# Attention and a two-layer product on one core: the second product's work listed one step further ahead

## The chip, the cores and the metric

The kernel runs on one core of one Trainium2 chip. The metric is the device time of one execution, in microseconds (us). The kernel before has a median of 1421.46 us in 3 runs (1420.41 to 1422.7).

## The reference

An attention with a threshold, then two matrix products with an activation between them. B = 8 batches, 8 heads, 576 positions, head size 64; the 8 heads side by side give x with 4608 tokens and 512 columns.

```python
scores = scale * np.matmul(q, k.transpose(0, 1, 3, 2))
thresh = np.max(scores, axis=-1, keepdims=True) - tau
scores = np.where(scores >= thresh, scores, -1000000000.0)
...
x = np.ascontiguousarray(attn_out.transpose(0, 2, 1, 3)).reshape(B * S, H * D)
h = x @ w_in                                   # 4608 x 512 by 512 x 2048
sp = np.where(h > 20.0, h, np.log1p(np.exp(np.minimum(h, 20.0))))
g = h * np.tanh(sp)
return (g @ w_out).astype(np.float32)          # 4608 x 2048 by 2048 x 512
```

w_in and w_out reach the chip as 64-bit words and are decoded to fp32 there.

## The kernel before

Each fp32 operand of a matrix product is split into a high part, a cast, and a low part, the rest, and three matmuls (high by high, high by low, low by high) stand for one. So every operand costs a cast on ACT (names that end in h) and a subtraction on DVE (names that end in l).

The program has two parts. In the first, up to about 970 us, attention runs tile by tile, and the first product h = x w_in (gemm1, L553) is woven into it, one batch behind. Its results go through PSUM and a staging tile hst (L582, four slices, two buffers in the pool xpool) to DRAM (hd). For the last batch gemm1 runs alone, as 32 units of 12 matmuls (L798 to L805). Into these units a table (steps, from L782) puts the decode of w_out in eight parts j: load_w, convert (ACT), compose (three DVE operations and one POOL addition, tiles s and a), upper_w (ACT, tile w2h), lower_w (DVE, tile w2l). It also puts there the first loads, activations and splits of the second part.

The second part is the loop at L849: 72 steps n, nine token groups c of 512 tokens by eight parts j of the inner dimension. Step n needs these pieces of work:

- load_z(n): two loads of 256 KB from hd into a tile z, on the queue of SP. Five buffers of z take turns (CYCLE).
- combine(n): the activation Mish of z on ACT (ACTIVATE z<-z 128x1024); from group 1 on also a DVE subtraction (z<-z 128x512) and two POOL subtractions (z<-z 128x256 each), which form combinations of the features.
- split_z(n): the cast gh on ACT and the rest gl on DVE, 128x1024 in group 0 and 128x1792 after it. Three buffers of gh and gl take turns by n % 3: one in the pool er, two in the pool wl, which is opened when gemm1 has ended.
- in group 0 only, sums_w(n) (four DVE operations 128x256, two shown as z<-s, one as z<-z,s and one as z<-s,z) and split_w(n) (sh on ACT, sl on DVE): combinations of the decoded weight, formed once and used by all later groups. They lie in the second half of the tile z of step n.
- the matmuls. Group 0 is a plain product, 24 matmuls 128x512 in a step. From group 1 on, seven products (PRODUCTS, L42) of combined weights and combined features stand for eight: 42 matmuls 128x256 in a step, those with sh and sl among them.

Outputs are collected in PSUM over the eight steps of a group, in eight banks that are taken in turn (bank, L773): four for group 0, seven for each later group. At a group's last step leave (L816) copies the first product's bank to a tile c on ACT, adds the others to it and to its like on DVE (c<-o,c) and stores four results on the queue of SP. Group 0 has two copies on ACT and two on DVE instead. The tiles c come from the pool wl, in six buffers (held, L811).

The class InOrder (L81) makes the order in which the program lists its instructions the order in which each engine runs them. So an instruction that waits holds back all that is listed after it for its engine. Since every operation of PE, DVE, ACT and POOL is recorded in its helper, the profile puts them all on one line, L91, and they are told apart by tile names and shapes. In the changed kernel the helper stands on L92.

In the loop, the order of listing for one step was this: for n < 8 sums_w(n), split_z(n+1), split_w(n), combine(n+2), load_z(n+3) and then the matmuls of step n; from n = 9 on split_z(n+2), combine(n+3), load_z(n+4), matmuls. At n = 8 the lead grows by one step.

Of the kernel before, what the change touches and what calls it, by code (L numbers as in the profile page):

```python
# [5 lines left out]
F32 = mybir.dt.float32  # L6
# [8 lines left out]
P = 128  # L15
# [20 lines left out]
HB = S // 2  # L36
# [2 lines left out]
QT = 256  # L39
NG = B * S // (2 * QT) * NJ  # L40
CYCLE = (3, 4, 2, 0, 1)
PRODUCTS = ((0, 1), (4, 5), (5, 3), (3, 4), (6, 0), (2, 6), (1, 2))  # L42
QCOL = {
    0: [(0, 0)],
# [70 lines left out]
class Decode:  # L115
# [31 lines left out]
    def add(self):  # L147
        self.nc.gpsimd.tensor_tensor(self.a, self.b, self.c, ALU.add)
# [8 lines left out]
def attention_moe(tc, q, k, v, tau, w_in, w_out, out):  # L157
# [3 lines left out]
    with ExitStack() as outer:  # L161
# [8 lines left out]
        back = cst.tile([P, 1], F32, name="back")  # L170

        homes = {"zp": zp}
        words = {}
        wa = {}
        ws = {}
# [90 lines left out]
        with ExitStack() as first:  # L266
# [6 lines left out]
            with ExitStack() as att:  # L273
# [279 lines left out]
                def gemm1(b, xs, bank=shared, first=1):  # L553

                    halves = (range(NF // 2), range(NF // 2, NF))
                    if b < B - 1:
                        order = [(c, f) for c in range(2) for fs in halves for f in fs]  # L560
                    else:
                        order = [(c, f) for fs in halves for c in range(2) for f in fs]
                    banks = {}
                    made = {}

                    def parts(c, f, ds):
                        if (c, f) not in banks:
                            banks[c, f] = bank("h")
                        h = banks[c, f]
                        half, at = divmod(f * P, DF // 2)  # L570
                        for d in ds:
                            xh, xl = xs[d][c]
                            wh, wl = (w[:, d, at:at + P] for w in w1[half])
                            for i, (a, m) in enumerate(((wh, xh), (wh, xl), (wl, xh))):
                                nc.tensor.matmul(
                                    h[:, :HB], a, m, start=d == 0 and i == 0, stop=d == ND - 1 and i == 2
                                )
                                yield

                    def leave(c, f):  # L580
                        if f % 4 == 0:
                            made["hst"] = xpool.tile([P, 4, HB], F32, name="hst", bufs=2)  # L582
                        hst, h = made["hst"], banks.pop((c, f))
                        if b < B - 1 or f % 2:
                            nc.scalar.copy(hst[:, f % 4], h[:, :HB])
                        else:
                            nc.vector.tensor_copy(hst[:, f % 4], h[:, :HB])
                        if f % 4 == 3:
                            store(nc.sync if b < B - 1 else nc.scalar, hst, (2 * b + c) * HB, f - 3)

                    for c, f in order[:first]:
                        yield from parts(c, f, range(ND - 1))
                    for n, (c, f) in enumerate(order):
                        steps = parts(c, f, range(ND - 1, ND) if n < first else range(ND))
                        for i in range(3 if n < first else 3 * ND):
                            next(steps)
                            if i == (2 if n < first else 3 * ND - 1):
                                leave(c, f)
                            yield
# [179 lines left out]

            homes["wr"] = wr  # L780
            steps = {}
            for j in range(NJ):  # L782
                u = 4 * j
                steps.setdefault(u, []).append((compose, j))
                steps.setdefault(u + 2, []).append((upper_w, j))
                steps.setdefault(u + 3, []).append((lower_w, j))
                if j >= 3:
                    steps.setdefault(u - 10, []).append((load_w, j))
                    steps.setdefault(u - 3, []).append((convert, j))
            for n, u in enumerate((19, 20, 24, 28, 31)):  # L790
                steps.setdefault(u, []).append((load_z, n))
            for n, u in enumerate((22, 26, 30)):
                steps.setdefault(u, []).append((combine, n))
            steps.setdefault(24, []).append((split_z, 0))
            for _ in stream:
                pass
            stream = gemm1(B - 1, batches[B - 1], bank, 4)
# [11 lines left out]
        places = out.rearrange("(n p) t -> p n t", p=P)  # L809

        def held():  # L811
            return wl.tile([P, 2, QT], F32, name="c", tag="c", bufs=6)

        sums = {}

        def leave(k, c, o):  # L816

            def put(value, n, half):
                at = (2 * c + half) * QT
                nc.sync.dma_start(places[:, 2 * n:2 * n + 2, at:at + QT], value)  # L820

            def add(to, a, b, op=ALU.add):
                nc.vector.tensor_tensor(to, a, b, op)

            if k == 0:
                sums["c"] = held()
                nc.scalar.copy(sums["c"], o)
            elif k == 1:
                sums["u"] = held()
                add(sums["u"], o, sums["c"])  # L830
            elif k == 2:
                sums["v"] = held()
                add(sums["v"], o, sums["u"])
            elif k == 3:
                value = held()
                add(value, o, sums["v"])
                put(value, 1, 1)
                add(sums["u"], o, sums["u"])
            elif k == 4:
                add(sums["u"], o, sums["u"])  # L840
                put(sums["u"], 0, 1)
            elif k == 5:
                add(sums["v"], sums["v"], o, ALU.subtract)
                put(sums["v"], 1, 0)
            else:
                add(sums["c"], o, sums["c"])
                put(sums["c"], 0, 0)

        for n in range(NG):  # L849
            c, j = divmod(n, NJ)  # L850
            if n < NJ:
                sums_w(n)
            for i in range(n + 1 + (n > NJ + 1), n + 2 + (n > NJ)):
                split_z(i)
            if n < NJ:
                split_w(n)
            for i in range(n + 2 + (n > NJ), n + 3 + (n >= NJ)):
                if i > 2:
                    combine(i)
            for i in range(n + 3 + (n >= NJ), n + 4 + (n >= NJ - 1)):  # L860
                if i > 4:
                    load_z(i)
            if j == 0:
                banks = [bank("o") for _ in range(4 if c == 0 else len(PRODUCTS))]
            if c == 0:
                gh, gl = (x.rearrange("p n t -> p (n t)") for x in gs.pop(n))
                wh, wlo = wa[j]
                order = [(e, d) for e in range(2) for d in range(ND)]
                if j == NJ - 1:
                    order.sort(key=lambda at: at[1])  # L870
                for e, d in order:
                    cols = slice(2 * e * QT + d * P, 2 * e * QT + (d + 1) * P)
                    toks = slice(2 * e * QT, 2 * (e + 1) * QT)
                    for i, (x, y) in enumerate(((wh, gh), (wh, gl), (wlo, gh))):
                        nc.tensor.matmul(
                            banks[d], x[:, cols], y[:, toks],
                            start=j == e == i == 0, stop=j == NJ - 1 and e == 1 and i == 2,
                        )
                    if j == NJ - 1 and e == 1:
                        value = held().rearrange("p n t -> p (n t)")  # L880
                        if d % 2:
                            nc.vector.tensor_copy(value, banks[d])
                        else:
                            nc.scalar.copy(value, banks[d])
                        nc.sync.dma_start(out[d * P:(d + 1) * P, :2 * QT], value)
                continue
            for k, (wi, gi) in enumerate(PRODUCTS):
                o = banks[k].rearrange("p (n t) -> p n t", t=QT)
                w, at = (wa[j], (0, 2, 3)[wi]) if wi < 3 else (ws[j], wi - 3)
                for b in range(2):  # L890
                    cols = slice(at * QT + b * P, at * QT + (b + 1) * P)
                    for i, (x, y) in enumerate(((0, 0), (0, 1), (1, 0))):
                        nc.tensor.matmul(
                            o[:, b], w[x][:, cols], gs[n][y][:, gi],
                            start=j == b == i == 0, stop=j == NJ - 1 and b == 1 and i == 2,
                        )
                if j == NJ - 1:
                    leave(k, c, o)
            gs.pop(n)
# [46 lines left out]
```

## Time and profile before

| | before |
|---|---|
| median of 3 runs | 1421.46 us |
| profiled execution | 1421.81 us |
| its span | 1420.0 us |
| mean granted TensorE clock | 0.976 |
| PE busy | 1345.4 us, 95% |
| DVE busy | 1102.4 us, 78% |
| ACT busy | 990.0 us, 70% |
| POOL busy | 837.0 us, 59% |

PE is TensorE, DVE VectorE, ACT ScalarE, POOL GpSimd; SP issues DMAs. A row of the timeline has the start, the duration in us, engine, line, operation, the tile written and the tiles read, shapes, a count, and in brackets how long the engine was idle before it and what ended that. A row of the list of waits has engine, tile and line, what released it, the total in us, the number of waits and the longest. A row of the groups of instructions has the count after the x, then busy us and mean ns, then idle us and its releasers. Successive operations of an engine overlap a little in the records, so that the distance between starts is what a chain of them takes.

In forty equal slices of the span, PE's busy share and the granted clock stand like this:

```profile
PE   9998899999999999999999999997998889889888
PEclk9999999999999999999999999998999999999999
```

### The profile page before, as it was taken

The numbers are of one execution on the slowest core, as the hardware profiler recorded it, in microseconds if no ns is written. First come the engines' busy times: TensorE is split into PE (matmuls) and PEld (weight loads), VectorE is DVE, ScalarE is ACT, GpSimd is POOL, SyncE is SP. The second block draws the span as 40 slices with busy tenths as digits, with TensorE's granted clock in tenths as the row PEclk, the third lists the DMA queues.
The fourth block names the chain that finished last, engine by engine and source line by source line (L and its number), as shares of the span: only waits on it lengthen the run. The fifth ranks groups of instructions, "written<-read, shape, count | busy, mean of one in ns | idle before, by whom it ended". The sixth has DMA issues, their size and how long they took to land. (4 is left out here: it accounts for less than half of the span.)

```text
span 1420.0 us, 29648 instructions
## 1 busy us (share of the span) xinstructions
PE 1345.4 (95%) x9799; PEld 1264.5 (89%) x9799; DVE 1102.4 (78%) x3018; ACT 990.0 (70%) x2052; POOL 837.0 (59%) x1191
## 2 busy tenths in 40 slices
PE   9998899999999999999999999997998889889888
PEld 6555899999999999999999999995898789879878
DVE  6999999999999999999999999557755545554554
ACT  5888878888888888888888888745544444443442
POOL 5778887878878778788788787332022222222221
PEclk9999999999999999999999999998999999999999
DMA  4333443333434334333333332165433323333330
GB/s 147 102 98 113 138 147 111 104 98 95 116 88 115 110 86 120 90 109 103 105 108 102 100 99 80 51 212 160 137 100 120 119 86 108 119 95 110 109 119 30
DMA packets 151912, 154.76 MB, mean 109 GB/s; under 512 B 35536, under 2 KB 128720, under 8 KB 151760
## 3 DMA queue, kind: packets, MB, share of 16 engines
q1 hardware_dynamic: 143312, 148.15, 35.1%
q10 hardware_dynamic: 8448, 4.72, 1.1%
q8 instruction: 78, 1.28, 0.4%
q14 instruction: 74, 0.61, 0.1%
HBM read 105.64 MB, written 47.19 MB: 108 GB/s over the span
## 5 line engine op out<-in xcount | busy, mean ns | idle before, releaser
L91 PE MATMUL h<-xh,w1h 128*128 128x288 f32 x1024 | 302.6, 296 | 2.3 <-ACT hst L91 1.9
L91 PE MATMUL h<-xl,w1h 128*128 128x288 f32 x1024 | 302.2, 295 | 0.0
L91 PE MATMUL h<-xh,w1l 128*128 128x288 f32 x1024 | 302.2, 295 | 0.0
L91 POOL TENSOR_TENSOR z<-z 128x256 f32<-128x256 f32 x128 | 94.3, 737 | 332.1 <-DVE z L91 319.9
L91 DVE TENSOR_TENSOR gl<-z,gh 128x1792 fp32r<-128x1792 f32 (+1 forms) x72 | 140.7, 1956 | 191.6 <-ACT gh L91 191.5
L91 POOL TENSOR_SCALAR p<-p,st 128x576 f32<-128x576 f32 x288 | 243.7, 846 | 58.1 <-DVE st L91 35.2
L91 ACT CAST gh<-z 128x1792 fp32r<-128x1792 f32 (+1 forms) x72 | 116.4, 1619 | 224.5 <-POOL z L91 210.1
L91 PE MATMUL s<-k,q 128*128 128x288 f32 (+1 forms) x1280 | 253.4, 323 | 8.4 <-DVE p L91 8.2
L91 DVE SCALAR_TENSOR_TENSOR p<-s,st,e 128x576 f32<-128x576 f32 x288 | 235.0, 816 | 20.3 <-ACT e L91 10.5
L91 ACT ACTIVATE e<-s,st 128x576 f32<-128x576 f32 x288 | 214.2, 744 | 36.2 <-DVE st L91 31.3
L91 DVE TENSOR_REDUCE st<-s 128x1 f32<-128x576 f32 x288 | 216.6, 752 | 2.8 <-PE s L91 2.7
L91 PEld LDWEIGHTS s<-k,q 128*128 128x128 f32 (+1 forms) x1280 | 181.5, 189 | 38.2 <-DVE p L91 23.6
L91 DVE TENSOR_TENSOR lo<-tp,hi 128x512 fp32r<-128x512 f32 (+1 forms) x280 | 174.7, 632 | 49.7 <-ACT hi L91 42.4
L91 PEld LDWEIGHTS h<-xh,w1h 128*128 128x128 f32 x1024 | 192.5, 188 | 3.3 <-ACT hst L91 2.5
L91 PEld LDWEIGHTS h<-xh,w1l 128*128 128x128 f32 x1024 | 192.4, 188 | 0.0
L91 PEld LDWEIGHTS h<-xl,w1h 128*128 128x128 f32 x1024 | 192.4, 188 | 0.0
L91 PE MATMUL o<-gh,sh 128*128 128x256 f32 x512 | 152.6, 298 | 32.7 <-ACT c L91 31.4
L91 PE MATMUL tp<-ident,p 128*128 128x128 f32 x1152 | 174.4, 274 | 3.7 <-DVE lo L91 2.5
L91 ACT CAST hi<-tp 128x512 fp32r<-128x512 f32 (+1 forms) x280 | 149.7, 545 | 35.9 <-PE tp L91 33.0
L91 PEld LDWEIGHTS tp<-ident,p 128*128 128x128 f32 x1152 | 138.9, 140 | 13.7 <-issue 5.4
L91 PE MATMUL o<-gh,sl 128*128 128x256 f32 x512 | 150.8, 294 | 0.0
L91 PE MATMUL o<-gl,sh 128*128 128x256 f32 x512 | 150.5, 294 | 0.0
(76 smaller groups left out, 3200.0 us busy)
## 6 DMA issues: line engine op xcount, KB each, us to landing
z<-hd SPq DMA_DIRECT2D x144, 256.0 KB, 3.1
r<-q SPq DMA_DIRECT2D x120, 160.0 KB, 2.3
r<-k SPq DMA_DIRECT2D x120, 160.0 KB, 2.3
out_t<-c SPq DMA_DIRECT2D x36, 256.0 KB, 2.4
r<-v SPq DMA_DIRECT2D x56, 160.0 KB, 2.3
dec<-w_in SPq DMA_DIRECT2D x32, 256.0 KB, 3.4
w<-w_out SPq DMA_DIRECT2D x16, 512.0 KB, 4.9
hd<-hst SPq DMA_DIRECT2D x12, 512.0 KB, 3.3
```

The costliest lines, as they stand in the source:

```text
L91: made = method(*args, **kwargs)
```

## The change

The diff touches three things. The table of the decode gets its own spacing (COMPOSE), 3.5 units on average where it was 4, and the first loads and activations move in it by up to three units. The staging tile hst moves from xpool to a pool of its own, hp, which the output tiles c share afterwards, two to a buffer. In the loop each step n now lists combine(n+3), then split_z(n+2) (at n = 0 also split_z(1)), then in group 0 sums_w(n) and split_w(n), then load_z(n+5), then the matmuls.

```diff
--- before.py
+++ after.py
@@ -39,6 +39,7 @@
 QT = 256
 NG = B * S // (2 * QT) * NJ
 CYCLE = (3, 4, 2, 0, 1)
+COMPOSE = (0, 3, 7, 10, 14, 17, 21, 24)
 PRODUCTS = ((0, 1), (4, 5), (5, 3), (3, 4), (6, 0), (2, 6), (1, 2))
 QCOL = {
     0: [(0, 0)],
@@ -170,6 +171,7 @@
         back = cst.tile([P, 1], F32, name="back")
 
         homes = {"zp": zp}
+        hp = outer.enter_context(tc.tile_pool(name="hp", bufs=2, side="left"))
         words = {}
         wa = {}
         ws = {}
@@ -579,7 +581,7 @@
 
                     def leave(c, f):
                         if f % 4 == 0:
-                            made["hst"] = xpool.tile([P, 4, HB], F32, name="hst", bufs=2)
+                            made["hst"] = hp.tile([P, 4, HB], F32, name="hst", tag="hst")
                         hst, h = made["hst"], banks.pop((c, f))
                         if b < B - 1 or f % 2:
                             nc.scalar.copy(hst[:, f % 4], h[:, :HB])
@@ -779,19 +781,22 @@
 
             homes["wr"] = wr
             steps = {}
-            for j in range(NJ):
-                u = 4 * j
-                steps.setdefault(u, []).append((compose, j))
-                steps.setdefault(u + 2, []).append((upper_w, j))
-                steps.setdefault(u + 3, []).append((lower_w, j))
+
+            def at(u, *work):
+                steps.setdefault(u, []).append(work)
+
+            for j, u in enumerate(COMPOSE):
                 if j >= 3:
-                    steps.setdefault(u - 10, []).append((load_w, j))
-                    steps.setdefault(u - 3, []).append((convert, j))
-            for n, u in enumerate((19, 20, 24, 28, 31)):
-                steps.setdefault(u, []).append((load_z, n))
-            for n, u in enumerate((22, 26, 30)):
-                steps.setdefault(u, []).append((combine, n))
-            steps.setdefault(24, []).append((split_z, 0))
+                    at(COMPOSE[j - 3] + 2, load_w, j)
+                    at(u - 2, convert, j)
+                at(u, compose, j)
+                at(u + 3, upper_w, j)
+                at(COMPOSE[j + 1] if j + 1 < NJ else u + 4, lower_w, j)
+            for n, u in enumerate((19, 20, 22, 25, 28)):
+                at(u, load_z, n)
+            for n, u in enumerate((22, 26, 29)):
+                at(u, combine, n)
+            at(24, split_z, 0)
             for _ in stream:
                 pass
             stream = gemm1(B - 1, batches[B - 1], bank, 4)
@@ -809,7 +814,8 @@
         places = out.rearrange("(n p) t -> p n t", p=P)
 
         def held():
-            return wl.tile([P, 2, QT], F32, name="c", tag="c", bufs=6)
+            pair = hp.tile([P, 2, 2, QT], F32, name="c", tag="hst")
+            return pair[:, 0], pair[:, 1]
 
         sums = {}
 
@@ -823,18 +829,16 @@
                 nc.vector.tensor_tensor(to, a, b, op)
 
             if k == 0:
-                sums["c"] = held()
+                sums["c"], sums["u"] = held()
                 nc.scalar.copy(sums["c"], o)
             elif k == 1:
-                sums["u"] = held()
                 add(sums["u"], o, sums["c"])
             elif k == 2:
-                sums["v"] = held()
+                sums["v"], sums["value"] = held()
                 add(sums["v"], o, sums["u"])
             elif k == 3:
-                value = held()
-                add(value, o, sums["v"])
-                put(value, 1, 1)
+                add(sums["value"], o, sums["v"])
+                put(sums["value"], 1, 1)
                 add(sums["u"], o, sums["u"])
             elif k == 4:
                 add(sums["u"], o, sums["u"])
@@ -848,18 +852,13 @@
 
         for n in range(NG):
             c, j = divmod(n, NJ)
+            combine(n + 3)
+            for i in range(n + 1 + (n > 0), n + 3):
+                split_z(i)
             if n < NJ:
                 sums_w(n)
-            for i in range(n + 1 + (n > NJ + 1), n + 2 + (n > NJ)):
-                split_z(i)
-            if n < NJ:
                 split_w(n)
-            for i in range(n + 2 + (n > NJ), n + 3 + (n >= NJ)):
-                if i > 2:
-                    combine(i)
-            for i in range(n + 3 + (n >= NJ), n + 4 + (n >= NJ - 1)):
-                if i > 4:
-                    load_z(i)
+            load_z(n + 5)
             if j == 0:
                 banks = [bank("o") for _ in range(4 if c == 0 else len(PRODUCTS))]
             if c == 0:
@@ -877,7 +876,9 @@
                             start=j == e == i == 0, stop=j == NJ - 1 and e == 1 and i == 2,
                         )
                     if j == NJ - 1 and e == 1:
-                        value = held().rearrange("p n t -> p (n t)")
+                        if d % 2 == 0:
+                            pair = [x.rearrange("p n t -> p (n t)") for x in held()]
+                        value = pair[d % 2]
                         if d % 2:
                             nc.vector.tensor_copy(value, banks[d])
                         else:
```

PE, DVE, ACT and POOL have as many instructions as before, and PE and POOL run theirs in the same order. DVE and ACT differ at three places.

First, DVE in the steady steps around the end of a token group (group 1 and the later ones). Before, as listed:

```order
L91 TENSOR_TENSOR gl<-z,gh 128x1792
L91 TENSOR_TENSOR z<-z 128x512
L91 TENSOR_TENSOR gl<-z,gh 128x1792
L91 TENSOR_TENSOR z<-z 128x512
L91 TENSOR_TENSOR gl<-z,gh 128x1792
L91 TENSOR_TENSOR z<-z 128x512
L91 TENSOR_TENSOR c<-o,c 128x512 x5
L91 TENSOR_TENSOR c<-c,o 128x512
L91 TENSOR_TENSOR c<-o,c 128x512
L91 TENSOR_TENSOR gl<-z,gh 128x1792
L91 TENSOR_TENSOR z<-z 128x512
```

After:

```order
L92 TENSOR_TENSOR gl<-z,gh 128x1792
L92 TENSOR_TENSOR z<-z 128x512
L92 TENSOR_TENSOR gl<-z,gh 128x1792
L92 TENSOR_TENSOR z<-z 128x512
L92 TENSOR_TENSOR gl<-z,gh 128x1792
L92 TENSOR_TENSOR z<-z 128x512
L92 TENSOR_TENSOR gl<-z,gh 128x1792
L92 TENSOR_TENSOR c<-o,c 128x512 x5
L92 TENSOR_TENSOR c<-c,o 128x512
L92 TENSOR_TENSOR c<-o,c 128x512
L92 TENSOR_TENSOR z<-z 128x512
```

What moved: z<-z of step n+3 now stands ahead of gl of step n+2, not behind it, and behind a group's output sums (c) a z<-z comes first.

Second, ACT at the end of a token group; COPY c is the copy of the group's first output. Before:

```order
L91 CAST gh<-z 128x1792
L91 ACTIVATE z<-z 128x1024
L91 CAST gh<-z 128x1792
L91 ACTIVATE z<-z 128x1024
L91 COPY c<-o 128x512
L91 CAST gh<-z 128x1792
L91 ACTIVATE z<-z 128x1024
```

After:

```order
L92 CAST gh<-z 128x1792
L92 ACTIVATE z<-z 128x1024
L92 CAST gh<-z 128x1792
L92 ACTIVATE z<-z 128x1024
L92 CAST gh<-z 128x1792
L92 COPY c<-o 128x512
L92 ACTIVATE z<-z 128x1024
```

What moved: the copy follows a cast gh where it followed an activation; the activation of step n+3 is now listed ahead of gh of step n+2.

Third, DVE and ACT in group 0. DVE, two steps in the middle of the group, before:

```order
L91 TENSOR_TENSOR sl_16029<-z,sh_16028 128x1024
L91 TENSOR_TENSOR z<-s 128x256 x2
L91 TENSOR_TENSOR z<-z,s 128x256
L91 TENSOR_TENSOR z<-s,z 128x256
L91 TENSOR_TENSOR gl<-z,gh 128x1024
L91 TENSOR_TENSOR sl_16069<-z,sh_16068 128x1024
L91 TENSOR_TENSOR z<-s 128x256 x2
L91 TENSOR_TENSOR z<-z,s 128x256
L91 TENSOR_TENSOR z<-s,z 128x256
L91 TENSOR_TENSOR gl<-z,gh 128x1024
```

After:

```order
L92 TENSOR_TENSOR gl<-z,gh 128x1024
L92 TENSOR_TENSOR z<-s 128x256 x2
L92 TENSOR_TENSOR z<-z,s 128x256
L92 TENSOR_TENSOR z<-s,z 128x256
L92 TENSOR_TENSOR sl_16081<-z,sh_16080 128x1024
L92 TENSOR_TENSOR gl<-z,gh 128x1024
L92 TENSOR_TENSOR z<-s 128x256 x2
L92 TENSOR_TENSOR z<-z,s 128x256
L92 TENSOR_TENSOR z<-s,z 128x256
L92 TENSOR_TENSOR sl_16121<-z,sh_16120 128x1024
```

What moved: gl, there of step n+1, stood between the sums (z<-s, z<-z,s, z<-s,z) and sl of the same step; now gl, of step n+2, stands ahead of that step's sums. ACT at the end of group 0, before:

```order
L91 ACTIVATE z<-z 128x1024
L91 CAST gh<-z 128x1024
L91 CAST sh_16265<-z 128x1024
L91 ACTIVATE z<-z 128x1024
L91 CAST gh<-z 128x1792
L91 CAST sh_16308<-z 128x1024
L91 ACTIVATE z<-z 128x1024
L91 COPY c<-o 128x512 x2
L91 CAST gh<-z 128x1792
```

After:

```order
L92 ACTIVATE z<-z 128x1024
L92 CAST gh<-z 128x1792
L92 CAST sh_16286<-z 128x1024
L92 ACTIVATE z<-z 128x1024
L92 CAST gh<-z 128x1792
L92 CAST sh_16329<-z 128x1024
L92 COPY c<-o 128x512 x2
L92 ACTIVATE z<-z 128x1024
L92 CAST gh<-z 128x1792
```

What moved: the two output copies of group 0 (COPY c) stood behind an activation and ahead of gh; now they stand directly behind the last sh.

## The prediction

> **What bounds the kernel now.** I read the stretches first: busy time of each engine (us, instructions), then the granted TensorE clock, the DMA share and GB/s.
>
> ```profile
> core 0: us, PE busy (x) PEld busy (x) DVE busy (x) ACT busy (x) POOL busy (x), PEclk, DMA share, GB/s
> 300.00:900.00 600.00, 599.96 (x4614) 592.51 (x4612) 552.97 (x1803) 510.88 (x1231) 481.28 (x732) 1.00 0.36 101
> ...
> 1300.00:1350.00 50.00, 43.99 (x350) 43.08 (x349) 25.39 (x23) 21.66 (x17) 12.29 (x18) 0.93 0.35 108
> ```
>
> To 900 us PE never rests, and the change leaves that part alone. Only the last 370 us, the second product from group 1 on, have a PE with pauses and a lower clock; there no other engine is even 60% busy, so something waits in a ring. The waits from 1030 us on, and then the rows of one step, name it:
>
> ```profile
> POOL z L91 <- DVE z L91: 277.3, 60, 5.8
> ACT gh L91 <- POOL z L91: 207.2, 60, 4.7
> DVE gl L91 <- ACT gh L91: 182.4, 54, 3.4
> PE o L91 <- ACT c L91: 31.4, 7, 4.5
> ...
> 1066.55 1.69 ACT L91 CAST gh<-z 128x1792 fp32r<-128x1792 f32 x1 [3.36 <-POOL z L91]
> 1068.28 2.02 DVE L91 TENSOR_TENSOR gl<-z,gh 128x1792 fp32r<-128x1792 f32 x1 [3.38 <-ACT gh L91]
> 1070.22 0.68 DVE L91 TENSOR_TENSOR z<-z 128x512 f32<-128x512 f32 x1
> 1070.98 1.52 POOL L91 TENSOR_TENSOR z<-z 128x256 f32<-128x256 f32 x2 [4.46 <-DVE z L91]
> 1072.54 1.68 ACT L91 CAST gh<-z 128x1792 fp32r<-128x1792 f32 x1 [3.34 <-POOL z L91]
> 1075.09 0.56 ACT L91 COPY c<-o 128x512 f32<-128x512 f32 x1
> 1075.70 0.58 PE L91 MATMUL o<-gh,sh 128*128 128x256 f32 x1 [4.48 <-ACT c L91]
> ```
>
> The ring: gh of one step (1066.55), its gl on DVE (1.73 later), the DVE subtraction z of the next step, listed behind that gl (1.94 later), its two POOL operations (0.76 later), and the next gh (1.56 later): 5.99 us a step, whatever PE does. The full chain of waits shows the same, POOL z twice and 4.4 us between, step after step. At the end of a token group the copy of the first output (COPY c) stands on ACT behind the ring too, and PE pauses 4.48 us for its bank. PE itself needs less:
>
> ```profile
> 1028.87 0.28 PE L91 MATMUL o<-gh,w2h 128*128 128x256 f32 x1
> 1029.57 0.28 PE L91 MATMUL o<-gh,sh 128*128 128x256 f32 x1
> 1034.52 0.28 PE L91 MATMUL o<-gh,sh 128*128 128x256 f32 x1
> 1039.49 0.28 PE L91 MATMUL o<-gh,sh 128*128 128x256 f32 x1
> 1414.73 0.28 PE L91 MATMUL o<-gh,w2l 128*128 128x256 f32 x1
> ```
>
> Rows two to four are the seventh matmul of steps 8, 9 and 10: 9.92 us for two steps of 42 matmuls, 4.96 a step, 0.118 a matmul, where the work was ready ahead. From 1039.49 to the last matmul, 62 steps took 375.2 us, 6.05 each. The ring and the pauses cost 62 × 1.09 = 68 us.
>
> **The change, part by part.** Instruction counts do not change on PE, DVE, ACT and POOL, and no kind of operation is new. So everything is a matter of order.
>
> **(1) Steps from group 1 on.** With z(n+3) listed ahead of gl(n+2), the operation behind gl(n+2) is z(n+4). The ring now runs gh(n+2), gl(n+2), z(n+4), POOL(n+4), gh(n+4): the same 5.99 us, but over two steps, 3.0 a step. So it no longer binds. Next is the busiest engine:
>
> ```profile
> L91 DVE TENSOR_TENSOR gl<-z,gh 128x1792 fp32r<-128x1792 f32 x64 | 129.4, 2024 | 183.5 <-ACT gh L91 183.4
> L91 DVE TENSOR_TENSOR z<-z 128x512 f32<-128x512 f32 x64 | 43.7, 684 | 0.0
> L91 DVE TENSOR_TENSOR c<-o,c 128x512 f32<-128x512 f32 x48 | 32.3, 687 | 4.2 <-PE o L91 1.7
> L91 ACT ACTIVATE z<-z 128x1024 f32<-128x1024 f32 x72 | 75.8, 1054 | 0.0
> ```
>
> DVE 2.02 + 0.68 + seven output sums of 0.69 per eight steps (0.60) = 3.3 us; ACT 1.69 + 1.05 + a copy of 0.56 per eight steps = 2.8; POOL 1.5; PE 4.96. PE is the bound. The pause at a group's end goes as well: ACT now has the copy behind gh(n+2), which starts when PE leaves step n-1's buffer, so copy and gh are done 1.69 + 0.56, about 2.3 us, into the group's last step, and PE wants that bank at 4.96 + 0.71 (six matmuls) = 5.7. The sums on DVE start at 1.73 + 1.94 = 3.7 into that step; the second of them is wanted at 7.1 and should end near 5.1. The z loads are listed one step earlier than before and cost nothing: they land beside 20 us of PE work; without that cover a late one would cost at most its few us once. The two POOL operations are the cover that can fail (rival B). SP's stores stand behind the sums, and a z load behind a store is issued about 3.7 us into the next step, more than a step ahead of its activation.
>
> **(2) Group 0 gets worse.** Here the listing before let sh(n) follow sums(n) without waiting for gl. Now a step's ACT order is Mish(n+3), gh(n+2), sh(n), and DVE's is gl(n+2), sums(n), sl(n), so that sh(n) waits for sums, sums for gl, gl for gh and gh for sh(n-1): one ring through both engines. Its pieces:
>
> ```profile
> 985.58 1.04 ACT L91 CAST gh<-z 128x1024 fp32r<-128x1024 f32 x1 [3.57 <-DMA hd<-hst]
> 986.66 1.23 DVE L91 TENSOR_TENSOR gl<-z,gh 128x1024 fp32r<-128x1024 f32 x1 [3.17 <-ACT gh L91]
> 987.80 1.22 DVE L91 TENSOR_TENSOR sl<-z,sh 128x1024 fp32r<-128x1024 f32 x1
> ...
> 990.51 1.04 ACT L91 CAST sh<-z 128x1024 fp32r<-128x1024 f32 x1 [1.99 <-DVE z L91]
> 991.46 1.06 ACT L91 ACTIVATE z<-z 128x1024 f32<-128x1024 f32 x1
> 992.55 1.05 ACT L91 CAST gh<-z 128x1024 fp32r<-128x1024 f32 x1
> 992.73 0.75 DVE L91 TENSOR_TENSOR z<-s 128x256 f32<-128x256 f32 x2
> 994.31 1.05 ACT L91 CAST sh<-z 128x1024 fp32r<-128x1024 f32 x1 [0.71 <-DVE z L91]
> ```
>
> sh to Mish 0.95, Mish to gh 1.09, gh to gl 1.08, gl to the next DVE operation 1.14, sums to sh 1.58: 5.84 us a step, against 3.80 (990.51 to 994.31) before. The steps that take in group 1's features cost more: gh and gl are 128x1792 there, 1.73 and 1.94 in place of 1.08 and 1.14, thus 7.29 for n = 6 and 7. And from n = 5 on the POOL pair falls on gl. What such an overlap costs, two pairs of rows bound:
>
> ```profile
> 969.20 2.40 POOL L91 TENSOR_TENSOR s<-s,w 128x1024 uint32<-128x1024 uint32 x1 [5.07 <-DVE s L91]
> 969.95 2.73 DVE L91 TENSOR_TENSOR gl<-z,gh 128x1024 fp32r<-128x1024 f32 x1 [0.89 <-ACT gh L91]
> ...
> 1016.43 1.29 DVE L91 TENSOR_TENSOR z<-s 128x256 f32<-128x256 f32 x2
> 1016.64 1.68 POOL L91 TENSOR_TENSOR z<-z 128x256 f32<-128x256 f32 x2 [36.96 <-DVE z L91]
> ```
>
> gl ran 2.73 instead of 1.23 beside a POOL operation, about until that one had ended; z<-s ran 1.29 instead of 0.75. So an overlap costs between nothing and the 1.5 of a whole POOL pair; I take the middle, 0.7, since POOL starts 0.2 to 0.9 us ahead of gl here. Then the eight sh are spaced 4 × 5.84 + 6.5 + 2 × 8.0 = 45.9 us.
>
> The start, and the first output copy of before:
>
> ```profile
> 980.80 1.22 DVE L91 TENSOR_TENSOR w2l<-s,w2h 128x1024 fp32r<-128x1024 f32 x1 [2.93 <-ACT w2h L91]
> ...
> 1024.87 0.59 ACT L91 COPY c<-o 128x512 f32<-128x512 f32 x1 [2.92 <-PE o L91]
> ```
>
> The first row is the last piece of the decode of w_out. After the change gh(1) no longer waits for the store of hst (the 3.57 above), whose memory its pool overlay; but ACT now has Mish(3) ahead of it, and the decode still ends at about 981 to 982, since each j waits for the one before in both orders. With the last copies of hst, Mish(2) and Mish(3) at 1.06 I put gh(1) at 985.4, as good as before. sh(0) follows gh(1) by gl(1), gl(2) and sums(0): 1.08 + 1.14 + 1.14 + 1.58 = 4.94, at 990.3; sh(7) comes at 1036.2, and behind it on ACT the first copy of group 0's output, 1037.2 to 1037.8. PE by itself would be through step 7 about when it was before, at 1028.87, or 2 us earlier. Step 8's first 24 matmuls have free banks, to 1031.7; the next one needs the bank which that copy frees. So PE waits 6 us from 1031.7 (8 if it came earlier), to 1037.8. Before, that copy ran at 1024.87, ahead of need. The decode's closer listing itself I cost at nothing, since PE's wait at step 8 hides what it moves; uncovered, it is worth up to 2 us either way.
>
> **(3) The clock after that wait.** PE's pauses in the present kernel lower the clock:
>
> ```profile
> 1076.09 0.41 PE L91 MATMUL o<-gl,sh 128*128 128x256 f32 x1
> 1076.30 0.41 PE L91 MATMUL o<-gh,sl 128*128 128x256 f32 x1
> 1081.33 0.33 PE L91 MATMUL o<-gh,sl 128*128 128x256 f32 x1
> ```
>
> After the pause of 4.48 us, matmuls follow 0.21 apart until 1081.33, 5.6 us from the restart: 5.6 × (1 - 0.118/0.21) = 2.5 us lost. I charge that once, and drop it at the seven group ends. The Trainium skill, "TensorE: Matmul & The Clock Gate", section "What's actually happening", has the full clock back after one busy window of about 3.4 us; by that the loss would be 1.5 us, an estimate, and the total 1 us lower. The row says longer, and I go by the row.
>
> **The sum.** Step 8 restarts at 1037.8 with 18 matmuls left, then 63 steps of 42: 2664 × 0.118 = 314.5; with 2.5 for the clock PE ends at 1354.8. Before it ended at 1414.73 + 0.12 = 1414.85. That is 60 us less. Behind PE's end stay the last sums and stores (span 1420.0, 5.15 us), and 1.8 us outside the span: the profiled execution took 1421.81, 0.35 over the median of 1421.46. So 1421.8 - 60 = **1362 us**.
>
> **Rivals.** *A, no wait at the end of group 0.* If sh(7) comes some 6 us earlier (POOL not disturbing DVE, an earlier gh(1)), the 6.1 and the 2.5 us go as well: 1353; with step 8 also 2 us earlier, 1351. For it: 2.1 of the 45.9 us are an assumed overlap. Against: without any overlap 43.8 remain, and 4 us of wait.
>
> *B, DVE and POOL in each other's way.* If every POOL pair held gl for its whole 1.53 us, DVE's chain in a step would be z 0.76, POOL 1.56, gl 1.94 and sums 0.6, with gaps about 5.1: 62 × 0.14 = 9 us more, 1371. Smaller pauses at group ends, where sums delay gl, give about the same, say 0.5 to 1 us at seven ends, and with a halved clock 2.5 more at each: up to 1385. Against: in the steady order POOL's pair should run just ahead of gl(n+2), which waits for PE. The Trainium skill, "SBUF — State Buffer", section "SBUF: two separate sides", says the port pair that DVE and GpSimd share is held for a whole instruction, also against a DVE operation with two inputs in SBUF; the 2.73 us agree. By it the sum would be that of B wherever the two do meet, and unchanged where gl comes later.
>
> *C, slower.* Running without pauses, PE is granted less clock from step 10 on. To cost the whole gain, 62 steps would have to last (375.2 - 8.6) / 62 = 5.91 us: that decides at a clock of 4.96 / 5.91 = 0.84; at 0.82 the time is about 1430. For: the 0.93 now. Against: that 0.93 comes from pauses, and 600 us without one had 1.00.
>
> *D, nothing changes*, because another order of the same ring holds, a z load or the buffers of the outputs: 1421. Against: every wait in the list above belongs to that one ring.
>
> **How the numbers follow.** The forecast, 1357 to 1367, has 0.60; A 0.15; B 0.21; C 0.02; D 0.02 (half of it within 0.2%, about what a measurement of this kernel can tell from no change, half a little faster). The range takes in A and most of B and leaves out its far end, C and D: 1350 to 1376. Faster 0.97, same 0.01, slower 0.02.
>
> **What would show it.** Right: PE starts steps 4.96 apart from about 1048 on, with a clock of 1.00 at group ends; gh waits for PE, not for POOL; the chain of waits is PE's; one wait of PE for ACT's copy, 6 to 8 us, at about 1030 to 1038. Wrong: gh waiting for POOL z in every step (D); gl longer than 2.02 with PE waiting for it (B); no such wait of PE (A); full stretches of PE at a clock under 0.9 (C).

## The result and the profile after

| | before | after |
|---|---|---|
| median of 4 runs | 1421.79 us | 1361.74 us (1360.85 to 1363.02) |
| span of the profiled execution | 1420.0 us | 1360.4 us |
| mean granted TensorE clock | 0.976 | 0.990 |
| PE busy | 95% | 97% |

The changed kernel takes 0.9579 of the time, 95% interval 0.9563 to 0.9596: 60.1 us less. The forecast was 1362 us, with a range of 1350 to 1376.

The same view by stretches of time, of the changed kernel (busy us of each engine, then granted clock, DMA share, GB/s):

```profile
300.00:900.00 600.00, 599.95 (x4613) 592.43 (x4612) 553.16 (x1802) 511.00 (x1230) 481.55 (x732) 1.00 0.36 101
...
1000.00:1050.00 50.00, 43.94 (x231) 38.15 (x230) 36.94 (x47) 26.60 (x26) 14.19 (x11) 0.93 0.41 128
1050.00:1100.00 50.00, 50.00 (x426) 50.00 (x426) 32.38 (x28) 27.07 (x22) 21.19 (x21) 1.00 0.42 133
...
1250.00:1300.00 50.00, 50.00 (x426) 50.00 (x426) 33.38 (x29) 26.88 (x21) 20.94 (x22) 1.00 0.43 134
```

The first part is what it was. From 1050 us on PE is busy without a gap and has its full clock, where before it had 44 of 50 us and 0.93. POOL is busy for 17 to 22 us of a full stretch, against 12 before. Part of that is the shorter step, which puts more of POOL's instructions into a stretch: 22 in the last row shown, against 18 in the prediction's row of before, would make 15 us at the old time of each. Where the rest comes from is taken up below, with experiment e7. The waits from 1030 us on:

```profile
POOL z L92 <- DVE z L92: 180.5, 48, 8.2
DVE gl L92 <- ACT gh L92: 98.9, 49, 2.7
ACT gh L92 <- issue: 73.3, 37, 2.3
ACT gh L92 <- POOL z L92: 59.0, 15, 5.3
```

PE is gone from the head of this list: in all of it PE has one wait left, for the output copy at 1038 us, and none for gl. gh waited for POOL 60 times, 207 us in all; now 15 times, 59 us. In 37 of the other cases the row says "issue", that is, nothing which the profile shows. The timeline (start, duration) tells what it was:

```profile
1099.63 2.02 DVE L92 TENSOR_TENSOR gl<-z,gh 128x1792 fp32r<-128x1792 f32 x1 [1.52 <-ACT gh L92]
1101.57 0.69 DVE L92 TENSOR_TENSOR z<-z 128x512 f32<-128x512 f32 x1
1102.33 1.57 POOL L92 TENSOR_TENSOR z<-z 128x256 f32<-128x256 f32 x2 [2.58 <-DVE z L92]
1102.57 1.69 ACT L92 CAST gh<-z 128x1792 fp32r<-128x1792 f32 x1 [2.02 <-issue]
1107.19 0.28 PE L92 MATMUL o<-gh,w2l 128*128 128x256 f32 x1
1107.55 1.70 ACT L92 CAST gh<-z 128x1792 fp32r<-128x1792 f32 x1 [2.33 <-issue]
...
1048.54 0.28 PE L92 MATMUL o<-gh,sh 128*128 128x256 f32 x1
1350.82 0.28 PE L92 MATMUL o<-gh,sh 128*128 128x256 f32 x1
```

The POOL pair of 1102.33 ends at 1103.90; the gh that uses it starts only at 1107.55, a step after the gh at 1102.57. The two gh are 4.98 us apart, PE's own step, and the second starts 0.08 us after the end of PE's last matmul of a step (1107.19 and 0.28): gh now waits for PE to leave a buffer. The last two rows are the seventh matmul of steps 10 and 71: 302.28 us for 61 steps, 4.955 each. The one wait of PE that is left:

```profile
1036.80 1.04 ACT L92 CAST sh<-z 128x1024 fp32r<-128x1024 f32 x1 [4.09 <-DVE z L92]
1037.75 1.07 ACT L92 COPY c<-o 128x512 f32<-128x512 f32 x2
1038.38 0.58 PE L92 MATMUL o<-gh,sh 128*128 128x256 f32 x1 [6.06 <-ACT c L92]
1043.12 0.38 PE L92 MATMUL o<-gh,w2h 128*128 128x256 f32 x1
```

It is step 8's fifth product, waiting for the bank that group 0's first output copy frees, and the copy stands directly behind the last sh. The last row ends a stretch of 4.74 us in which matmuls follow 0.21 us apart.

### The profile page after: what moved, and what is told of

Same layout as the page of the kernel before. It is cut to its first block, busy times and chain, and to the rows that moved or that the text cites. A ratio compares the mean times of both kernels' runs of the same rounds, so it can differ in the third digit from the quotient of the medians.

```text
span 1360.4 us, 29638 instructions
## 1 busy us (share of the span) xinstructions
PE 1322.8 (97%) x9799; PEld 1249.2 (92%) x9799; DVE 1112.4 (82%) x3018; ACT 989.4 (73%) x2052; POOL 874.3 (64%) x1191
## 4 chain that ended last, share of the span: by engine, by line
PE 85%; DVE 6%; ACT 5%; issue 2%; POOL 1%; DMA 1%; ACTq 0%; DVEq 0%; SPq 0%; POOLq 0%
PE h L92 26%; PE o L92 23%; PE s L92 13%; PE y L92 12%; PE tp L92 9%; PE t L92 1%; DVE z L92 1%; DVE st L92 1%; DVE gl L92 1%; DVE p L92 1%; POOL s L92 1%; DVE dec L92 1%; ACT gh L92 1%; ACT e L92 1%; ACT w L92 1%
## 5 line engine op out<-in xcount | busy, mean ns | idle before, releaser
L92 POOL TENSOR_TENSOR z<-z 128x256 f32<-128x256 f32 x128 | 130.3, 1022 | 226.4 <-DVE z L92 221.4
L92 PE MATMUL o<-gh,sh 128*128 128x256 f32 x512 | 144.0, 281 | 6.1 <-ACT c L92 6.1
L92 POOL TENSOR_TENSOR x<-x,yo 64x256 f32<-64x256 f32 (+1 forms) x112 | 89.8, 802 | 89.5 <-ACT yo L92 86.3
L92 PE MATMUL o<-gh,sl 128*128 128x256 f32 x512 | 144.7, 283 | 0.0
```

The source lines that it names most:

```text
L92: made = method(*args, **kwargs)
```

## The experiments

The theory: the order of the steady steps alone carries the gain, since it lets the ring gh, gl, z, POOL, gh span two steps; the new order in group 0 costs something, for sh there waits for gl. The main rival: the gain comes from supply, that is from the earlier loads, the pool of the outputs or the spacing of the decode. Each comparison is with the kernel before on the same chip.

**One part alone, or one part undone.** e1_steady_order:

```diff
--- before
+++ e1_steady_order
         for n in range(NG):
             c, j = divmod(n, NJ)
+            if n > NJ:
+                combine(n + 3)
             if n < NJ:
                 sums_w(n)
...
-                if i > 2:
+                if 2 < i < NJ + 4:
                     combine(i)
```

> The kernel before, with one edit: from step 9 on combine(n+3) is listed ahead of split_z. Ring theory: this order alone frees the steady steps, and group 0 keeps its old order and does not hold PE, so PE runs 62 steps at 4.96 us from 1038.75 on: about 1353 us (1351 to 1356). Rival, supply: what helps is the earlier loads, the pool of the outputs or the decode's spacing, and the order alone gives little: 1410 to 1422 us.

Measured: 1353.63 us against 1422.02, ratio 0.9521 (0.9505 to 0.9537). The order of the steady steps alone brings 68 us, more than the whole change. The supply rival falls.

e2_group0_undone:

```diff
--- after
+++ e2_group0_undone
-            combine(n + 3)
+            if n < NJ:
+                sums_w(n)
+            else:
+                combine(n + 3)
             for i in range(n + 1 + (n > 0), n + 3):
                 split_z(i)
             if n < NJ:
-                sums_w(n)
                 split_w(n)
+                combine(n + 3)
```

> The changed kernel, with group 0 listed as before (sums_w ahead of the splits, the activation last), everything else kept, its lead too. Ring theory: sh no longer waits for gl, PE's wait of 6.1 us for the output copy at step 8 goes, and the half clock behind it (2.5 us): 1352 to 1355 us. Rival: that wait comes from the late start of group 0 and stays: 1360 to 1363 us.

Measured: 1350.26 us, ratio 0.9501 (0.9486 to 0.9515), so 11.5 us less than the changed kernel, and 1.7 us below the range expected. The trace of this run has no wait of PE at step 8: its first matmuls, 128x256, run on behind those of step 7, and its 25th, the last row, follows the 24th at once, where the changed kernel waits 6.06 us:

```profile
1025.23 0.39 PE L92 MATMUL o<-gh,w2l 128*128 128x512 f32 x1
1025.46 0.28 PE L92 MATMUL o<-gh,w2h 128*128 128x256 f32 x1
...
1028.15 0.28 PE L92 MATMUL o<-gh,sl 128*128 128x256 f32 x1
1028.27 0.28 PE L92 MATMUL o<-gh,sh 128*128 128x256 f32 x1
```

The order of group 0 is what made PE wait. It cost more than the 8.6 us foreseen, because the start of the group is slower as well: from PE's first matmul of step 0 to the seventh of step 8 it is 977.50 to 1026.15 here, 48.65 us, and 979.10 to 1030.04 in the changed kernel, 50.94, before its wait.

e3_steady_undone, the opposite of e1:

```diff
--- after
+++ e3_steady_undone
-            combine(n + 3)
+            if n < NJ:
+                combine(n + 3)
             for i in range(n + 1 + (n > 0), n + 3):
                 split_z(i)
             if n < NJ:
                 sums_w(n)
                 split_w(n)
+            else:
+                combine(n + 3)
```

> The changed kernel, with the order of the steps from n = 8 on put back (split_z(n+2) ahead of combine(n+3)); table, staging, loads and group 0 as changed. Ring theory: 6.0 us a step again, and group 0's later end (gh of step 10 and later some 6 to 8 us late) on top: 1427 to 1432 us, slower than before. Rival, supply: the rest of the change carries the gain: under 1390 us.

Measured: 1430.31 us, ratio 1.0062 (1.0047 to 1.0077). All of the change but the steady order is a loss of 8.3 us. The list of waits from 1045 us on is the one of before, nearly to the digit, and the wait at step 8 is there too:

```profile
1038.16 0.58 PE L92 MATMUL o<-gh,sh 128*128 128x256 f32 x1 [6.37 <-ACT c L92]
...
POOL z L92 <- DVE z L92: 277.0, 60, 5.8
ACT gh L92 <- POOL z L92: 210.8, 61, 4.7
DVE gl L92 <- ACT gh L92: 182.6, 54, 3.4
PE o L92 <- ACT c L92: 31.4, 7, 4.5
```

e4_table_staging is the kernel before with the COMPOSE table, the pool hp and the pairs of outputs, the loop untouched.

```diff
--- before
+++ e4_table_staging
+            for j, u in enumerate(COMPOSE):
...
-                            made["hst"] = xpool.tile([P, 4, HB], F32, name="hst", bufs=2)
+                            made["hst"] = hp.tile([P, 4, HB], F32, name="hst", tag="hst")
...
-            return wl.tile([P, 2, QT], F32, name="c", tag="c", bufs=6)
+            pair = hp.tile([P, 2, 2, QT], F32, name="c", tag="hst")
+            return pair[:, 0], pair[:, 1]
```

> The kernel before, with the changed table of the decode and the staging and outputs in their own pool; the loop as before. Ring theory: the start of group 0 moves by a few us, which the ring behind it hides or passes on: 1419 to 1424 us. Rival, supply: a good part of the gain lies here: under 1410 us.

Measured: 1419.47 us, ratio 0.9985 (0.9976 to 0.9995): about 2.5 us. e10_staging_alone has the last two pieces of that diff only:

> The kernel before with the staging and the outputs in their own pool alone; the decode's table and the loop as before. gh(1) no longer waits 3.57 us for the store of hst, so group 0 from step 1 on and all behind it come 2 to 3 us earlier: 1418.5 to 1420 us, and the decode's closer spacing is worth nothing. Rival, the 2.5 us of e4_table_staging come from the spacing: 1421 to 1423 us here.

Measured: 1419.30 us against 1422.38, ratio 0.9983 (0.9974 to 0.9992), in 11 runs. So the pool alone gives all of it, and the spacing nothing that these runs can tell. Its trace has gh(1) at 983.39, where the kernel before had 985.58 behind the 3.57 us of waiting for the store of hst, and PE's wait for that gh is 2.64 us where it was 5.04:

```profile
983.39 1.04 ACT L91 CAST gh<-z 128x1024 fp32r<-128x1024 f32 x1 [1.00 <-ACT hst L91]
984.49 0.50 PE L91 MATMUL o<-gh,w2h 128*128 128x512 f32 x1 [2.64 <-ACT gh L91]
```

The parts add up: -68.4 (e1) - 2.5 (e4) + 11.5 (what e2 saves on the whole) makes -59.4, and the whole change is -60.1. Without the first term it is +9.0, and e3 has +8.3.

**The ring made longer.** In e5 and e6 the cast gh is done twice from step 10 on; the result is the same.

```diff
-                nc.scalar.copy(to[0], y)
+                for _ in range(2 if n > NJ + 1 else 1):
+                    nc.scalar.copy(to[0], y)
```

> The kernel before with the cast gh done twice from step 10 on (1.6 us more of ACT in a step, same result). Ring theory: the ring of one step grows from 6.0 to 7.6 us and 62 steps last 99 us longer: 1515 to 1525 us. Rival, the steps before are held by something else (the outputs' bank, the z loads): under 1450 us, since ACT is busy 2.8 of 6 us.

> The changed kernel with the cast gh done twice from step 10 on. Ring theory: the ring now spans two steps, 7.6 us for 9.9 us of PE, and ACT has 4.3 us of work in a step of 4.96; so nothing changes but some tenths of a us at group ends, where the output sums come 1.6 us later: 1361 to 1367 us. Rival, the ring still closes over one step and was only shortened below PE's 4.96 us: 1400 us or more.

Measured: the kernel before goes to 1523.59 us (two runs, 1522.76 to 1524.42), 102 us more; the changed kernel to 1369.44 (1365.26 to 1369.98), 8 us more. The same 1.6 us in a step cost 62 times in the one kernel (99 us) and hardly at all in the other: ACT had no room in the ring of one step, and has it in the ring of two. e6 ends 2.4 us above what was expected of it. In a group's last step the sums on DVE come later, and PE waits for them; the list of waits and one of its rows:

```profile
PE o L92 <- DVE c L92: 3.6, 7, 0.5
1082.05 0.35 PE L92 MATMUL o<-gh,sh 128*128 128x256 f32 x1 [0.52 <-DVE c L92]
```

With each such wait the step behind a group's end lasts 5.9 to 6.0 us instead of 4.96, seven times.

**DVE and POOL in each other's way.** e7 does the two POOL subtractions twice from step 12 on.

```diff
-                    nc.gpsimd.tensor_tensor(y[:, 6], y[:, 1], y[:, 5], ALU.subtract)
-                    nc.gpsimd.tensor_tensor(y[:, 7], y[:, 6], y[:, 3], ALU.subtract)
+                    for _ in range(2 if n > NJ + 3 else 1):
+                        nc.gpsimd.tensor_tensor(y[:, 6], y[:, 1], y[:, 5], ALU.subtract)
+                        nc.gpsimd.tensor_tensor(y[:, 7], y[:, 6], y[:, 3], ALU.subtract)
```

> The changed kernel with the two POOL subtractions done twice from step 12 on (1.55 us more of POOL in a step, same result). If DVE and POOL exclude each other for whole instructions, a step needs 1.94 + 0.7 of DVE and 3.1 of POOL one after the other, 5.8 us, and 60 steps last 50 us longer: 1400 to 1420 us. If they run beside each other, POOL's 3.1 us fit into 4.96: 1361 to 1368 us.

Measured: 1408.28 us (two runs, 1408.19 to 1408.36), 46.5 us over the changed kernel, 0.78 a step on average. POOL's 3.1 us of work would fit into a step of 4.96 if DVE left it alone; that it does not, the timeline of e7 shows:

```profile
1200.66 9.99 POOL L92 TENSOR_TENSOR z<-z 128x256 f32<-128x256 f32 x8 [0.63 <-DVE z L92]
1201.80 2.31 DVE L92 TENSOR_TENSOR gl<-z,gh 128x1792 fp32r<-128x1792 f32 x1 [1.21 <-ACT gh L92]
1204.03 1.23 DVE L92 TENSOR_TENSOR z<-z 128x512 f32<-128x512 f32 x1
1207.61 2.45 DVE L92 TENSOR_TENSOR gl<-z,gh 128x1792 fp32r<-128x1792 f32 x1 [2.35 <-ACT gh L92]
1212.41 2.31 DVE L92 TENSOR_TENSOR gl<-z,gh 128x1792 fp32r<-128x1792 f32 x1 [1.21 <-ACT gh L92]
```

Eight subtractions of 0.74 us alone, 5.9 in all, take 9.99, and the DVE operations beside them 2.31, 1.23 and 2.45 where 2.02, 0.68 and 2.02 are usual: the two engines take turns, operation by operation. The Trainium skill, "SBUF — State Buffer", section "SBUF: two separate sides", has this as a lock on the port pair that both share, held for a whole instruction; e7 agrees with it.

The time lies in the range expected, but not by the step that was expected. From 1201.80 to 1212.41 two steps take 10.61 us, 5.3 each and not 5.8. PE does not even run them at that pace: between group ends nearly all its steps still take 4.95 to 4.97 us, and what the others fall behind is paid at the ends of the groups, where PE waits for ACT's output copy (15.9 us in all) and for the sums on DVE (10.3 us) and runs at a lower clock after it.

**A faster kernel.** What is left in e2 is the start of group 0, where PE waits 5.2 us ahead of step 0. In e8 the last part of the decode is listed after the last result copies of gemm1, its cast and rest in step 2; in e9 one place later still.

```diff
--- e2_group0_undone
+++ e8_last_decode_later
-                at(u, compose, j)
+                if j < NJ - 1:
+                    at(u, compose, j)
...
+            compose(NJ - 1)
+            load_z(4)
...
                 split_w(n)
+                if n == 2:
+                    upper_w(NJ - 1)
+                    lower_w(NJ - 1)
                 combine(n + 3)
```

> Group 0 listed as in e2_group0_undone, and the last part of the decode (j = 7, needed only at step 7) listed after gemm1's last result copies, its cast and rest in step 2; load_z(4) behind it. If the wait of PE of 5.2 us ahead of step 0 comes from result copies that stand behind compose(7) and gl(0) on DVE and behind w2h(7) on ACT, group 0 starts some 5 us earlier and gh(1) too: 1342 to 1347 us. Rival, the start is held by the load and activation of z or by memory of gemm1: 1349 to 1352 us.

> e8_last_decode_later with compose(7) and load_z(4) one place later still, behind split_w(0): in e8 PE waited 2.55 us at step 1 for a gl that stood behind sums_w(0), which ran 2.99 us beside the POOL addition of the decode. If that is the cause, about 2.5 us go: 1344 to 1346 us. Rival, another wait takes its place (z(4) now comes later, gh(1) sets step 1): 1347 to 1350 us.

Measured: e8 1347.54 us, ratio 0.9485 (0.9471 to 0.9499); e9 1347.26, ratio 0.9471 (0.9458 to 0.9484). In e8 PE waits 2.6 us ahead of step 0, half of what it did, and the time is 0.5 us above the range expected. e9 gains nothing that can be told from e8, as its rival said: the wait that it aimed at goes, and another takes its place. In e8 a DVE pair runs beside the POOL addition of the decode and lasts 2.99 us instead of 0.75, with gl(1) behind it; in e9 PE waits only 0.37 us there, but at step 8 it waits 0.42 and 1.05 us for the output copies instead:

```profile
979.85 2.99 DVE L92 TENSOR_TENSOR z<-s 128x256 f32<-128x256 f32 x2
980.07 2.49 POOL L92 TENSOR_TENSOR s<-s,w 128x1024 uint32<-128x1024 uint32 x1 [7.66 <-DVE s L92]
984.83 0.71 PE L92 MATMUL o<-gl,w2h 128*128 128x512 f32 x1 [2.55 <-DVE gl L92]
...
1024.84 0.39 PE L92 MATMUL o<-gh,sh 128*128 128x256 f32 x1 [0.42 <-ACT c L92]
1026.86 0.39 PE L92 MATMUL o<-gh,w2h 128*128 128x256 f32 x1 [1.05 <-DVE c L92]
```

The first three rows are of e8, the last two of e9. Both are 14 us faster than the changed kernel.

## Why the prediction was right

**The ring over two steps** held, in kind and in size: 4.955 us a step against 4.96, no pause at a group's end, the clock at 1.00. e1, e3, e5 and e6 show that the order does it. Two readings of the kernel before were loose. The 375.2 us begin at a step's seventh matmul and so hold 61.8 steps, not 62: 6.07 us each, and 68.5 us lost; the sum does not use them. And that mean hides how PE lost the time: most of its steps took 4.95 to 5.0 us before, too, but around the end of group 1 three took 5.75, 10.66 and 7.84 (seventh matmuls at 1059.30, 1065.05, 1075.70 and 1083.55). PE, faster than the ring by a us a step, caught up with it by the end of each group and paid there, waiting for the copy and then running at a lower clock.

**Group 0's ring and PE's wait** held: the wait was foreseen at 6 us, from 1031.7 to 1037.8, and it is 6.06, until 1038.38. But three terms under it were off and made up for each other, so that the agreement to some tenths of a us is in part luck. The spacing of sh is 5.70 us in a plain step, not 5.84:

```profile
1003.25 1.05 ACT L92 CAST sh<-z 128x1024 fp32r<-128x1024 f32 x1 [2.75 <-DVE z L92]
1008.95 1.05 ACT L92 CAST sh<-z 128x1024 fp32r<-128x1024 f32 x1 [2.75 <-DVE z L92]
```

gh follows Mish by 0.96 here; the 1.09 came from a place where gh had needed that very Mish, and now it needs an older one. Second, sh(0) came at 991.85, not 990.3, as gh(1) started at 986.93 and not at 985.4. Third, the overlap with POOL: I charged gl 0.7 us for it, but gl kept its time, and POOL and the sums behind gl paid:

```profile
1024.42 3.25 POOL L92 TENSOR_TENSOR z<-z 128x256 f32<-128x256 f32 x2 [4.10 <-DVE z L92]
1025.06 2.03 DVE L92 TENSOR_TENSOR gl<-z,gh 128x1792 fp32r<-128x1792 f32 x1 [0.71 <-ACT gh L92]
1027.00 1.29 DVE L92 TENSOR_TENSOR z<-s 128x256 f32<-128x256 f32 x2
```

gl gets in between POOL's two operations and holds back the second, which in turn holds z<-s: 1.29 instead of 0.75. So steps 6 and 7 have 7.68 us each (8.0 charged) and step 5 6.79 (6.5 charged).

**The clock** was charged 2.5 us; 4.74 us at a spacing of 0.21 make 4.74 × (1 - 0.118/0.21) = 2.1.

**The sum**: PE ends at 1354.94 + 0.12 = 1355.06, forecast 1354.8.

**Staging costed at nothing** was the weakest step. The wait for the store of hst is worth 2 to 3 us (e10), and the prediction set gh(1) "as good as before". In the changed kernel that was nearly so, since Mish(3) and late result copies took the wait's place (ACT's rows from 983.27 to 986.93); with the old order of group 0 it is a gain. Likewise the loss from group 0's order is 11.5 us (e2), of which the sum had 8.6; the 2.3 us at the group's start stood only in A, as an earlier step 8.

**The rivals.** A did not happen in this kernel, but e2 is its case: 1350.26 us, near the 1351 worked out for it with an earlier step 8. B's mechanism is real here, but its price was not paid: the engines do hold each other up, gh waits for POOL 15 times, up to 5.3 us, and PE never waits for gl from step 10 on, since the two steps of lead take it in. e7 shows that with twice POOL's work the lead no longer does. Nothing of C: 300 us of PE without a pause kept a clock of 1.00. D falls with the time and with the waits of gh, which the ring no longer makes in every step.

## What to carry to other kernels

With engines that run in listed order, look at what an instruction stands behind as much as at what it needs. A subtraction for the next step listed behind this step's last one closed a ring over three engines, each half idle, and moving one call by one place opened it. And the same reordering must be read again in each phase of the loop: in the steps where other work (here the sums of the weight) sits in the same queues, it tied a new ring that took back a sixth of the gain.

## What the runs showed of the hardware

DVE and POOL take turns even where neither is near full: a POOL pair of 1.55 us became 3.2 beside one gl, and from 1050 to 1350 us one POOL subtraction took 1.00 us on average in the changed kernel, where it had taken 0.73 in the steady steps before. POOL's busy time then holds waiting: of the 21 us in which it is busy in a stretch of 50, about 15 are work.
